# Block-sparse attention and a gated feed-forward layer in one kernel: another order of the same work

## The chip, the cores and the metric

The kernel runs on one core of a Trainium2 chip. Times are microseconds of device time; three runs are shown. In the tables PE is TensorE (PEld its weight loads), DVE is VectorE, ACT is ScalarE, POOL is GpSimd and SP is SyncE, which here issues every DMA.

## The reference

```python
# q, k, v: (8, 8, 576, 64); heads 0-3 local, heads 4-7 strided
scores = (q @ k.T) / sqrt(64)
rel = pos[:, None] - pos[None, :]
mask_local   = (rel >= 0) & (rel < 32)
mask_strided = (rel >= 0) & (pos[None, :] % 32 == pos[:, None] % 32)
scores = where(mask, scores, -1e9)
attn = exp(scores - max) / (sum(exp(scores - max)) + 1e-9)
x = (attn @ v).transpose(0, 2, 1, 3).reshape(4608, 512)
h = x @ w_in                                # 512 -> 2048
g = h * erf(softplus(h))
out = g @ w_out                             # 2048 -> 512
```

The inputs are float32; the weights reach the kernel as 64-bit words.

## The kernel before, in words

**The feed-forward part.** The 4608 tokens are cut into 12 chunks of 384, three for each pair of batches, and the 2048 hidden columns into 16 f-tiles of 128. `ftile(k)` is one f-tile of one chunk, k from 0 to 191. `mm1` (12 matmuls, L708) makes a 128 x 384 tile `h` in one of three PSUM buffers. The gate is evaluated by a chain that alternates between ScalarE and VectorE: `n1` (ScalarE), `n2` (VectorE, a<-h,a), `n3`, `n4` (ScalarE), `n5` (VectorE, a<-a,h), `n6` (VectorE, b<-b,a: both inputs in SBUF), `n7`, `gate` (ScalarE), `prod` (VectorE, h<-b,h), `split_hi` (ScalarE, ghi), `split_lo` (VectorE, glo, L749). After `split_lo` the h buffer is free. Three `mm2` (three matmuls each, L778) then add the f-tile's part to the outputs o0, o1 and o2; with the last f-tile of a chunk these are copied out and stored. A fp32 product is formed from high and low parts, so x, g and the weights are all kept as a pair. Names carry the f-tile's number: `glo_92` is the low part of f-tile 92.

**The attention part.** `piece` handles one pair of heads, one part j (0 to 2) of the sequence, for batches 0 and 1, whose work stands at the start. `quad` handles two pairs of heads for batches 2 to 7, and is named batch_headpair_j: 3_0_0 is batch 3, local heads, j = 0, and 5_2_0 is batch 5, strided heads, j = 0. I call them loc and str. A quad's scores (L484, 32 small matmuls in the trace) fill two PSUM banks; the banks have 384 columns in loc quads, 504 in str quads, and str quads with j = 2 have one bank of 288. For each bank: `mask` (VectorE, L502, one input in PSUM), `maxi` (GpSimd, an all-reduce over partitions, mx, L510), `sub` (VectorE, L517, sm<-sm,mx, both inputs in SBUF), `exp` (ScalarE, L524), `total` (GpSimd, all-reduce of sums, su, L530). The sums are transposed, inverted and spread by VectorE; `av` (x<-sm,v, TensorE, L574) needs the two `exp`; `scale`, `split_hi` and `split_lo_x` write the chunk's x.

**The order.** Nothing in the code above sets when an instruction stands where. Each op is added to a `Plan` with an engine, a cost in us, a key, the ops it follows and the buffers it uses. `Plan.order` is a list scheduler: for each engine it looks at the first WINDOW ops by key, finds when each could start, and takes the earliest, and among those about equally early the one with the lowest key. `new` buffers are taken from a pool of fixed depth, so an op that needs a buffer waits for the last user of the one that it replaces. Where TensorE would have nothing to do before the first mm1, a small `warm` matmul is put in. For the SBUF port that VectorE and GpSimd share the plan has a lock: a `sub`, an `n6` and some weight ops may not start while an op of GpSimd holds it, which is until its end less `FREED`:

```python
TWO = {"n6", "sub", "bits0", "bits1", "bits2", "split_lo_w"}
FREED = {"maxi": 0.75, "total": 0.95}
self.locks = eng == "pool" or eng == "dve" and emit.__name__ in TWO
```

The keys come from some 40 constants at the head of the file (SLOT is the key distance of f-tiles, MM2 the lag of mm2 in slots, W1K to W2S place the weights, A0 and A1 the pieces, QE, QO and QD the quads). The engines run the list in order, each waiting on semaphores where it needs another; the costs are of the plan alone.

**The weights.** w_in and w_out are loaded in 32 blocks (L653), and each is converted by three VectorE ops, a ScalarE copy and a VectorE subtraction. All of this is ahead of f-tile 16. `words8` to `words11` are the blocks that f-tiles 8 to 11 use.

Of the kernel before, what the change touches and what calls it, by code (L numbers as in the profile page):

```python
# [25 lines left out]
SW = 512  # L26


PRO = 78.728118
SLOT = 7.9300244  # L30
MM2 = 12.39792
W1K = (6.53644, 49.1778, -5.03539, 71.3026)
W1S = (5.65989, 16.7449, 3.18762, 26.1391)
W2K = 63.715556
W2S = 9.812094
A0K = -3.8060487
A0S = 1.2281868
A0D = 24.083007
A1K = 112.4806
A1S = -4.9858923  # L40
A1D = -8.5092613
QE = (12.856, 11.4352, 31.5648, 4.72851)
QO = (-4.21485, 2.52639)
QD = (0.348349, 1.45887, 1.7431, 1.71864, 1.13326)
ASH = 2.896798
ADT = 2.7828178
BACKLOG = 1.6450532

QL = 96
RB = 7  # L50
# [43 lines left out]

TWO = {"n6", "sub", "bits0", "bits1", "bits2", "split_lo_w"}

FREED = {"maxi": 0.75, "total": 0.95}


class Op:  # L100
# [9 lines left out]
class Plan:  # L110
# [5 lines left out]
    SAME = {"pe": 0.0, "act": 0.14, "dve": 0.13, "pool": 0.1, "sp": 0.0}  # L116
    LATENCY = {"pe": 0.25, "act": 0.2, "dve": 0.15, "pool": 0.6, "sp": 0.1}
    PATIENCE = 0.002
    WINDOW = 60

    def __init__(self, bufs):
        self.bufs, self.ops, self.filler = bufs, [], None
# [1 line left out]
    def add(self, eng, dur, key, emit, after=(), new=(), use=(), earliest=0.0):  # L124
        op = Op(eng, dur, key, emit, after, new, use, earliest)
        self.ops.append(op)
        return op
# [17 lines left out]
    def order(self):  # L145
# [4 lines left out]
        while left:  # L150
            best = None
            for e in self.ENGINES:
                can = [(o, n, self._ready(o, live)) for n, o in enumerate(queue[e][: self.WINDOW])]
                floor = max(free[e], dma - BACKLOG) if e == "sp" else free[e]
                port = held.get({"dve": "pool", "pool": "dve"}.get(e), 0.0)
# [34 lines left out]
def attention_moe(  # L190
# [37 lines left out]
    def buf(pool, tag, shape, name, dtype=F32):  # L228
        def make():
            return pools[pool].tile(shape, dtype, tag=tag, name=name, bufs=bufs[tag])  # L230

        return Buf(tag, make)

    def named(name, f):
        f.__name__ = name
        return f
# [178 lines left out]
    def quad(b, loc, j, key, dt, ring):  # L415
# [9 lines left out]
        cols = 4 * w // nbank  # L425
# [4 lines left out]
        sm = [buf("apool", "sm", [P, 512], f"sm{i}_{pid}") for i in range(nbank)]  # L430
        mx = [buf("apool", "mx", [P, 512], f"mx{i}_{pid}") for i in range(nbank)]
        su = [buf("apool", "mx", [P, 512], f"su{i}_{pid}") for i in range(nbank)]
# [95 lines left out]
        def total(k):  # L528
            def run():
                yield nc.gpsimd.partition_all_reduce(su[k][:, :cols], sm[k][:, :cols], P, ReduceOp.add)  # L530

            return named("total", run)
# [75 lines left out]
        add = plan.add  # L608
# [4 lines left out]
        o_e = []  # L613
        for k in range(nbank):
            o = add("dve", dve(cols), key + 0.1 + 0.01 * k, mask(k), [o_s], [], [s[k], sm[k]])
            o = add("pool", 0.4 + cols * 0.0028, key + 0.2 + 0.01 * k, maxi(k), [o], [mx[k]], [sm[k]], earliest=6.7)
            o = add("dve", dve(cols), key + QD[0] * dt + 0.01 * k, sub(k), [o], [], [mx[k], sm[k]])
            o_e.append(add("act", act(cols), key + QD[0] * dt + 0.1 + 0.01 * k, exp(k), [o], [], [sm[k]]))
        o_g = []
        for k in range(nbank):  # L620
            o = add("pool", 0.5 + cols * 0.005, key + QD[1] * dt + 0.01 * k, total(k), [o_e[k]], [su[k]], [sm[k]])
            o_g.append(o)
        n_g = (1 if pos == n else 2 * nblk) * 0.06 + width / 960.0 + (0.06 if pos > n else 0.0)
        o = None
        for h in range(2):
            k = h % nbank
            o = add("dve", n_g, key + QD[2] * dt + 0.01 * h, gather(h), [o_g[k]] + ([o] if o else []), [tt, inv] if h == 0 else [], [su[k], tt])
        o = add("dve", 0.36, key + QD[2] * dt + 0.05, invert, [o], [rc], [tt])
        o_i = add("dve", dve(width), key + QD[2] * dt + 0.06, spread, [o], [], [rc, inv])
        d_v = (1.2 if n > QL else 0.98) if nblk == 2 else 0.6  # L630
# [3 lines left out]
        for i in range(2):  # L634
            hi, lo = split(i)
            o = add("act", act(w, 0.06), key + QD[4] * dt + 0.1, hi, [o_x] + ring, [], [px])
# [57 lines left out]
    def ftile(k, ready):  # L694

        c, f = k // NFC, k % NFC
        v0 = PRO + SLOT * k
        ph = buf("ps_h", "h", [P, 512], f"h_{k}")
        a = buf("mpool", "a", [P, CH], f"a_{k}")
        bb = buf("mpool", "b", [P, CH], f"b_{k}")  # L700
        ghi = buf("mpool", "ghi", [P, CH], f"ghi_{k}", F32R)
# [49 lines left out]
        add = plan.add  # L751
        ta, tp, td = act(CH), act(CH, 0.05), dve(CH)

        def at(offset):
            return v0 + (offset + 0.3) * SLOT / 3.9

        first = add("pe", 2.09, v0, mm1, ready[0], [ph])
        o = add("act", tp, at(0.0), n1, [first], [a], [ph])
        o = add("dve", td, at(0.6), n2, [o], [], [ph, a])
        o = add("act", ta, at(1.2), n3, [o], [], [a])  # L760
        o = add("act", ta, at(2.25), n4, [o], [bb], [a])
        o = add("dve", td, at(2.9), n5, [o], [], [a, ph])
        o = add("dve", td, at(3.5), n6, [o], [], [a, bb])
        o = add("act", ta, at(4.35), n7, [o], [], [bb])
        o = add("act", ta, at(5.55), gate, [o], [], [bb])
        o = add("dve", td, at(6.2), prod, [o], [], [bb, ph])
        o_h = add("act", tp, at(6.8), split_hi, [o], [ghi], [ph])
        o_l = add("dve", td, at(7.9), split_lo, [o_h], [glo], [ph, ghi])
        last = []
        for t in range(NTT):  # L770
# [4 lines left out]
            def mm2(t=t, po=po):  # L775
# [7 lines left out]
            o = add(  # L783
                "pe", 0.693, v0 + MM2 * SLOT + 0.2 * t, mm2, [o_l] + ready[1] + ([order_o[t]] if f else []),
                [po] if f == 0 else [], [ghi, glo] + ([] if f == 0 else [po]),
            )
            order_o[t] = o
            last.append(o)
            if f == NFC - 1:
# [7 lines left out]

                o = add("act", act(DM, 0.06), v0 + 2.5 * SLOT + 0.7 + 0.2 * t, evac, [o], [ob], [po])
                add("sp", P * DM * 4 / 3.6e5, o.key + 0.1, store, [o], [], [ob])
# [17 lines left out]
    o = plan.add("sp", 0.6, -20.0, load_consts, new=[con_f])  # L817
# [2 lines left out]
    o_ps, order_o = [None] * NTT, [None] * NTT  # L820

    x_of = {}
    mm1_of, mm1_first = {}, []

    w1, w2, win, wout = [], [], [], []
    for f in range(0, DF, SW):
        for c in range(NCC):
            i = len(w1)
            rows, sl = slice(c * P, (c + 1) * P), slice(f, f + SW)
            op, pair = weight(i, w_in, rows, sl, W1K[i // 4] + W1S[i // 4] * (i % 4))  # L830
            w1.append(op)
            win.append(pair)
    for f in range(NFC):
        rows, sl = slice(f * P, (f + 1) * P), slice(0, DM)
        op, pair = weight(NFC + f, w_out, rows, sl, W2K + W2S * f)
        w2.append(op)
# [57 lines left out]
    first = plan.add("pe", 0.11, -10.0, warm, o_con, [warm_ps])  # L894
# [102 lines left out]
```

## Time and profile before

| | before |
|---|---|
| three runs, median (lowest to highest) | 976.35 us (975.68 to 977.12) |
| the profiled execution | 977.93 us |
| its span, first to last instruction | 976.2 us |
| PE busy | 950.1 us, 97% |
| DVE busy | 796.0 us, 82% |
| ACT busy | 652.8 us, 67% |
| POOL busy | 327.4 us, 34% |
| granted TensorE clock | 1.00 |
| DMA | 68.86 MB, most of it in the first 80 us |

Busy is time in which an engine has an instruction in it; a matmul that waits inside the pipeline is counted busy. The span is 1.7 us shorter than the profiled time, for what lies around it. In the rows that follow, "PEld h L708 <- DVE glo L749: total, times, longest" is a wait: who, at which line, waited for whom. A row of the timeline begins with the start and the length in us.

### The profile page before, as it was taken

How to read it: one execution, taken by the hardware profiler on the slowest of the kernel's cores; microseconds unless marked ns; L12 is line 12 of the kernel's file. 1: busy time of each engine (PE TensorE's matmuls, PEld its weight loads, DVE VectorE, ACT ScalarE, POOL GpSimd, SP SyncE). 2: the span in 40 equal slices, each digit the busy share in tenths (PEclk: the TensorE clock that was granted, in tenths of full speed). 3: DMA queues.
4: the chain of work that ended last, by engine and by line, in shares of the span. 5: the costliest groups of instructions: out<-in, count | busy, mean ns of one | idle time of the engine just before them, and what ended most of it. 6: DMA issues, size and time to landing. Idle time of an engine off the chain costs nothing.

```text
span 976.2 us, 16572 instructions
## 1 busy us (share of the span) xinstructions
PE 950.1 (97%) x6052; PEld 823.8 (84%) x6052; DVE 796.0 (82%) x1727; ACT 652.8 (67%) x1475; POOL 327.4 (34%) x160
## 2 busy tenths in 40 slices
PE   8999999999999999999999999999999999999998
PEld 6788888888878888888887888888887888999997
DVE  6999999787888887777888798778788888666664
ACT  3777777667667666667656766766766766766765
POOL 3533115234453552243454544313445344000000
PEclk9999999999999999999999999999999999999999
DMA  8994202112122121102121211111212210000000
GB/s 311 323 363 128 68 1 76 38 44 70 52 57 77 46 71 47 42 26 83 39 81 52 70 55 48 65 37 44 70 35 74 76 46 4 33 1 1 33 1 34
DMA packets 37666, 68.86 MB, mean 71 GB/s; under 512 B 4176, under 2 KB 18640, under 8 KB 37584
## 3 DMA queue, kind: packets, MB, share of 16 engines
q1 hardware_dynamic: 37584, 67.80, 21.6%
q8 instruction: 48, 0.79, 0.3%
q14 instruction: 34, 0.28, 0.1%
HBM read 58.34 MB, written 9.44 MB: 69 GB/s over the span
## 4 chain that ended last, share of the span: by engine, by line
PE 53%; DVE 32%; ACT 10%; issue 3%; DMA 2%; SPq 0%; DVEq 0%
PE h L708 25%; PE o L778 22%; DVE a L713 6%; DVE b L713 5%; DVE glo L749 4%; ACT b L716 4%; DVE h L743 3%; ACT a L716 3%; DVE sm L517 2%; PE x L574 1%; DVE sm L502 1%; PE s L484 1%; DVE tt L548 1%; DMA qk<-qk_loc 1%; DVE w L666 1%
## 5 line engine op out<-in xcount | busy, mean ns | idle before, releaser
L778 PE MATMUL o<-pair,ghi 128*128 128x512 f32 x1152 | 363.1, 396 | 0.0
L708 PE MATMUL h<-xhi,pair 128*128 128x384 f32 x1536 | 306.1, 341 | 13.1 <-DVE glo L749 12.6
L708 PEld LDWEIGHTS h<-xhi,pair 128*128 128x128 f32 x1536 | 266.4, 188 | 39.1 <-DVE glo L749 30.1
L716 ACT ACTIVATE b<-b 128x384 f32<-128x384 f32 x384 | 199.8, 524 | 83.9 <-DVE b L713 80.7
L778 PEld LDWEIGHTS o<-pair,ghi 128*128 128x128 f32 x1152 | 209.8, 188 | 39.9 <-issue 2.0
L778 PE MATMUL o<-pair,glo 128*128 128x512 f32 x576 | 224.6, 390 | 0.0
L510 POOL PARTITION_ALL_REDUCE mx<-sm x66 | 102.0, 1588 | 360.3 <-DVE sm L502 357.3
L530 POOL PARTITION_ALL_REDUCE su<-sm x66 | 183.4, 2807 | 66.8 <-ACT sm L524 66.8
L708 PE MATMUL h<-xlo,pair 128*128 128x384 f32 x768 | 164.5, 336 | 0.0
L716 ACT ACTIVATE a<-a 128x384 f32<-128x384 f32 x192 | 100.9, 525 | 77.3 <-DVE a L713 75.2
L713 DVE SCALAR_TENSOR_TENSOR a<-a,h 128x384 f32<-128x384 f32 x192 | 104.9, 546 | 52.8 <-ACT b L716 51.6
L749 DVE TENSOR_TENSOR glo<-h,ghi 128x384 fp32r<-128x384 f32 x192 | 105.2, 548 | 42.5 <-ACT ghi L746 41.4
L708 PEld LDWEIGHTS h<-xlo,pair 128*128 128x128 f32 x768 | 136.1, 188 | 0.0
L743 DVE TENSOR_TENSOR h<-b,h 128x384 f32<-128x384 f32 x192 | 105.8, 554 | 31.7 <-ACT b L716 31.1
L778 PEld LDWEIGHTS o<-pair,glo 128*128 128x128 f32 x576 | 108.2, 188 | 23.6
L713 DVE SCALAR_TENSOR_TENSOR b<-b,a 128x384 f32<-128x384 f32 x192 | 126.5, 660 | 1.8
L713 DVE SCALAR_TENSOR_TENSOR a<-h,a 128x384 f32<-128x384 f32 x192 | 105.4, 549 | 21.5 <-ACT a L716 20.8
L716 ACT ACTIVATE a<-h 128x384 f32<-128x384 f32 x192 | 93.0, 485 | 39.2 <-PE h L708 38.2
L746 ACT CAST ghi<-h 128x384 fp32r<-128x384 f32 x192 | 90.5, 472 | 38.3 <-DVE h L743 19.8
L716 ACT ACTIVATE b<-a 128x384 f32<-128x384 f32 x192 | 100.2, 522 | 2.9
L313 POOL PARTITION_ALL_REDUCE mx<-sm x24 | 41.7, 1739 | 65.5 <-ACT sm L305 62.0
L517 DVE TENSOR_TENSOR sm<-sm,mx 128x384 f32<-128x384 f32 (+2 forms) x66 | 52.1, 790 | 0.4
(53 smaller groups left out, 695.8 us busy)
## 6 DMA issues: line engine op xcount, KB each, us to landing
qk<-qk_loc SPq DMA_DIRECT2D x48, 304.0 KB, 3.3
qk<-qk_str SPq DMA_DIRECT2D x32, 380.0 KB, 3.7
v<-v_all SPq DMA_DIRECT2D x80, 130.0 KB, 2.2
out<-ob SPq DMA_DIRECT2D x36, 256.0 KB, 2.1
words<-w_in SPq DMA_DIRECT2D x16, 512.0 KB, 6.0
words<-w_out SPq DMA_DIRECT2D x16, 512.0 KB, 6.4
qk<-qk_str SPq DMA_DIRECT2D x16, 136.0 KB, 2.5
v<-v_all SPq DMA_DIRECT2D x16, 65.0 KB, 2.0
```

Of the source, the lines that this page charges most:

```text
L313: yield nc.gpsimd.partition_all_reduce(mx[:, :cols], sm[:, :cols], P, ReduceOp.max)
L484: yield nc.tensor.matmul(s[bank][cols_k, c : c + n], qk[i][rows, keys + part * 64 : keys + (part + 1) * 64], qk[i][rows, (blk * 2 + h) * n ...
L510: yield nc.gpsimd.partition_all_reduce(mx[k][:, :cols], sm[k][:, :cols], P, ReduceOp.max)
L517: yield nc.vector.tensor_tensor(out=d, in0=d, in1=mx[k][:, :cols], op=ALU.subtract)
L530: yield nc.gpsimd.partition_all_reduce(su[k][:, :cols], sm[k][:, :cols], P, ReduceOp.add)
L708: yield nc.tensor.matmul(ph[:, :CH], win[4 * s + cc][:, w, fs], x[cc][:, c0 : c0 + CH], start=(i == 0), stop=(i == len(terms) - 1))
L713: yield nc.vector.scalar_tensor_tensor(out=out, in0=in0, scalar=scalar, in1=in1, op0=op0, op1=op1)
L716: yield nc.scalar.activation(dst, src, func, bias=bias[i], scale=scale)
L743: yield nc.vector.tensor_tensor(out=ph[:, :CH], in0=bb.tile, in1=ph[:, :CH], op=ALU.mult)
L746: yield nc.scalar.copy(ghi.tile, ph[:, :CH])
L749: yield nc.vector.tensor_tensor(out=glo.tile, in0=ph[:, :CH], in1=ghi.tile.bitcast(F32), op=ALU.subtract)
L778: yield nc.tensor.matmul(po.tile, g[:, ts], wout[f][:, w], start=(f == 0 and i == 0), stop=(f == NFC - 1 and i == 2),)
```

## The change

Three things are edited, and all act through the order alone. The cost of `total` in the plan, and how early it gives up the port, are set anew. Two dependences are added to the plan: `mm1` of an f-tile follows the mm1 before it, and `split_hi` follows the split_hi before it. All key constants have new values, and the scheduler looks 70 ops ahead instead of 60. The instructions themselves are the same; line numbers from 757 on move by one or two.

```diff
-PRO = 78.728118
-SLOT = 7.9300244
-MM2 = 12.39792
+PRO = 78.092106
+SLOT = 5.9116753
+MM2 = 25.630719
...
-FREED = {"maxi": 0.75, "total": 0.95}
+FREED = {"maxi": 0.7, "total": 1.0}
...
-    WINDOW = 60
+    WINDOW = 70
...
-            o = add("pool", 0.5 + cols * 0.005, key + QD[1] * dt + 0.01 * k, total(k), [o_e[k]], [su[k]], [sm[k]])
+            o = add("pool", 0.094 + cols * 0.0063, key + QD[1] * dt + 0.01 * k, total(k), [o_e[k]], [su[k]], [sm[k]])
...
-        first = add("pe", 2.09, v0, mm1, ready[0], [ph])
+        first = add("pe", 2.09, v0, mm1, ready[0] + mm1_first[-1:], [ph])
...
-        o_h = add("act", tp, at(6.8), split_hi, [o], [ghi], [ph])
+        o_h = add("act", tp, at(6.8), split_hi, [o] + hi_of[-1:], [ghi], [ph])
+        hi_of.append(o_h)
...
-    mm1_of, mm1_first = {}, []
+    mm1_of, mm1_first, hi_of = {}, [], []
```

What it moves, at three places. On VectorE, around the two `sub` of quad 5_2_0 (`sm0` and `sm1` are its two banks), before:

```order
L713 SCALAR_TENSOR_TENSOR a_93_5947<-a_93_5947,h_93_5914 128x384
L517 TENSOR_TENSOR sm0_5_2_0_5892<-sm0_5_2_0_5892,mx0_5_2_0_5939 128x504
L713 SCALAR_TENSOR_TENSOR b_93_5970<-b_93_5970,a_93_5947 128x384
L749 TENSOR_TENSOR glo_92_5998<-h_92_5831,ghi_92_5994 128x384
L517 TENSOR_TENSOR sm1_5_2_0_5893<-sm1_5_2_0_5893,mx1_5_2_0_5963 128x504
L604 TENSOR_TENSOR xlo2_82<-x_4_2_2_5942,xhi2_78 128x18x4
```

and in the changed kernel:

```order
L713 SCALAR_TENSOR_TENSOR b_94_5997<-b_94_5997,a_94_5978 128x384
L517 TENSOR_TENSOR sm0_5_2_0_5960<-sm0_5_2_0_5960,mx0_5_2_0_6000 128x504
L749 TENSOR_TENSOR glo_93_6037<-h_93_5908,ghi_93_6033 128x384
L517 TENSOR_TENSOR sm1_5_2_0_5961<-sm1_5_2_0_5961,mx1_5_2_0_6017 128x504
L743 TENSOR_TENSOR h_94_5939<-b_94_5997,h_94_5939 128x384
```

The `n6` (b<-b,a) that stood between the subs now stands ahead of the first, and one row is left between them.

On TensorE, ahead of the `av` of quad 3_0_1 (x_3_0_1): before, the last rows of the second of two mm1 (f-tile 51) stand there, behind two mm1 and five mm2 after the quad's scores:

```order
L708 MATMUL h_51_3659<-xlo0_80,pair0_293 128x384
L708 MATMUL h_51_3659<-xlo1_81,pair1_329 128x384
L708 MATMUL h_51_3659<-xlo2_82,pair2_383 128x384
L708 MATMUL h_51_3659<-xlo3_83,pair3_420 128x384
L574 MATMUL x_3_0_1_3680<-sm0_3_0_1_3579,v0_3_0_1_3394 64x96
```

and in the changed kernel, after one mm2, the mm1 of f-tile 50 and these five mm2 behind the scores:

```order
L708 MATMUL h_50_3619<-xlo3_83,pair3_523 128x384
L779 MATMUL o1_2_2847<-pair30_1920,ghi_46_3537 128x512 x2
L779 MATMUL o1_2_2847<-pair30_1920,glo_46_3540 128x512
L779 MATMUL o2_2_2876<-pair30_1920,ghi_46_3537 128x512 x2
L779 MATMUL o2_2_2876<-pair30_1920,glo_46_3540 128x512
L779 MATMUL o0_2_2837<-pair31_1972,ghi_47_3605 128x512 x2
L779 MATMUL o0_2_2837<-pair31_1972,glo_47_3608 128x512
L779 MATMUL o1_2_2847<-pair31_1972,ghi_47_3605 128x512 x2
L779 MATMUL o1_2_2847<-pair31_1972,glo_47_3608 128x512
L779 MATMUL o2_2_2876<-pair31_1972,ghi_47_3605 128x512 x2
L779 MATMUL o2_2_2876<-pair31_1972,glo_47_3608 128x512
L574 MATMUL x_3_0_1_3679<-sm0_3_0_1_3586,v0_3_0_1_3260 64x96
```

The `av` has moved ahead of the mm1 of f-tile 51 and stands closer to its scores.

On SP, at the start of the program, before:

```order
L806 DMA con_f_87<-consts 128x446
L653 DMA words8_89<-w_in 128x1024
L268 DMA qk_0_0_0_91<-qk_loc 128x608
L275 DMA v_0_0_0_93<-v_all 128x260
L268 DMA qk_0_1_0_95<-qk_loc 128x608
L275 DMA v_0_1_0_97<-v_all 128x260
L653 DMA words9_101<-w_in 128x1024
```

and in the changed kernel:

```order
L807 DMA con_f_87<-consts 128x446
L268 DMA qk_0_0_0_89<-qk_loc 128x608
L275 DMA v_0_0_0_91<-v_all 128x260
L268 DMA qk_0_1_0_93<-qk_loc 128x608
L275 DMA v_0_1_0_95<-v_all 128x260
L275 DMA v_0_0_1_97<-v_all 128x260
L653 DMA words11_101<-w_in 128x1024
```

The first block of weights has moved behind the inputs of two pieces and the v of a third. The pieces of batch 1, which were spread over f-tiles 0 to 10, j = 2 first, are now spread over f-tiles 0 to 15, j = 0 first. On TensorE the last rows, from the mm1 of f-tile 158 on, stand as before.

More of the change, by code (lines that the diff above doesn't have):

```diff
@@ L26 @@
 SW = 512
-PRO = 78.728118
-SLOT = 7.9300244
-MM2 = 12.39792
[L32 to L47, printed above, removed]
+PRO = 78.092106
+SLOT = 5.9116753
+MM2 = 25.630719
+W1K = (30.3392, 45.2407, 29.777, 74.3109)
+W1S = (6.66747, 15.6958, -3.12843, 8.62929)
+W2K = 80.64347
+W2S = 6.6022671
+A0K = 0.61635903
+A0S = 4.0703236
+A0D = -2.7259218
+A1K = 77.691688
+A1S = 7.4559608
+A1D = -4.9661421
+QE = (13.0906, 7.59449, 28.6735, 3.97592)
+QO = (-2.73583, 2.28537)
+QD = (0.569358, 2.08749, 1.61931, 1.79434, 1.13453)
+ASH = -0.34305701
+ADT = -0.58951321
+BACKLOG = 1.9815506
 QL = 96
```

## The prediction

> **What bounds the kernel now.** I read the page's first part, then the windows by stage, then the waits, then the timeline at the longest waits.
>
> ```profile
> PE 950.1 (97%) x6052; PEld 823.8 (84%) x6052; DVE 796.0 (82%) x1727; ACT 652.8 (67%) x1475; POOL 327.4 (34%) x160
> 0.00:50.40 50.40, 45.27 (x322) 35.55 (x322) 41.07 (x89) 28.61 (x84) 23.09 (x17) 1.00 0.93 319
> 50.40:150.00 99.60, 96.59 (x596) 84.32 (x596) 99.33 (x228) 74.29 (x170) 26.33 (x16) 1.00 0.40 134
> 200.00:826.00 626.00, 613.26 (x4089) 527.59 (x4088) 524.97 (x1151) 412.33 (x926) 258.12 (x121) 1.00 0.18 55
> ...
> 50.37 0.95 PE L708 MATMUL h<-xhi,pair 128*128 128x384 f32 x4
> ```
>
> The columns of the windows are length, then busy time of PE, PEld, DVE, ACT and POOL, granted clock, DMA share, GB/s. TensorE is the engine that sets the time, in three stages. Until the first mm1 (50.37), the DMA queues (0.93) and VectorE prepare weights. Until 150 us VectorE is never idle (99.33 of 99.6 us). From 200 to 826 us, f-tiles and quads mixed, VectorE works 84% of the time and nothing but TensorE is full. So what an order of work can win is TensorE's waiting. These are its waits from 150 to 826 us, and the first row for 50 to 150 us:
>
> ```profile
> PEld h L708 <- DVE glo L749: 2.6, 6, 0.8
> ...
> PEld h L708 <- DVE glo L749: 27.5, 46, 1.7
> PEld x L574 <- ACT sm L524: 2.6, 5, 0.7
> ```
>
> The weight load of the next mm1 waits 27.5 us in all for `split_lo` (glo), the last op on an h buffer: there are three h buffers, so mm1 of f-tile k+3 waits until the chain of f-tile k has ended. Why is that chain late? Two VectorE ops have a long tail, the others none:
>
> ```profile
> L713 DVE SCALAR_TENSOR_TENSOR a<-h,a x192: 494/551/559, 53.8 to 962.9; 128x384 f32<-128x384 f32 x192
> L713 DVE SCALAR_TENSOR_TENSOR b<-b,a x192: 493/551/2564, 57.0 to 966.4; 128x384 f32<-128x384 f32 x192
> L517 DVE TENSOR_TENSOR sm<-sm,mx x66: 457/559/2647, 144.3 to 817.2; 128x384 f32<-128x384 f32 x36, 128x504 f32<-128x504 f32 x24, 128x288 f32<-128x288 f32 x6
> ...
> L713 DVE SCALAR_TENSOR_TENSOR b<-b,a 128x384 f32<-128x384 f32 x192 | 126.5, 660 | 1.8
> ```
>
> Minimum, median and maximum: `n6` (b<-b,a) and `sub` (sm<-sm,mx) reach 2.6 us where their medians are 0.55. Both read two SBUF tiles; `n2` (a<-h,a) has one input in PSUM and stays at 0.559. The timeline shows what holds them, in quad 3_2_0 (batch 3, strided heads, j=0) and then 4_2_0:
>
> ```profile
> 282.39 0.68 DVE L517 TENSOR_TENSOR sm<-sm,mx 128x504 f32<-128x504 f32 x1
> 283.92 2.65 DVE L517 TENSOR_TENSOR sm<-sm,mx 128x504 f32<-128x504 f32 x1
> 283.82 3.19 POOL L530 PARTITION_ALL_REDUCE su<-sm  x1 [2.27 <-ACT sm L524]
> 287.28 1.08 PE L574 MATMUL x<-sm,v 128*64 128x126 f32 x14 [0.41 <-ACT sm L524]
> ...
> 426.28 6.52 POOL L530 PARTITION_ALL_REDUCE su<-sm  x2 [1.11 <-ACT sm L524]
> 426.50 2.56 DVE L713 SCALAR_TENSOR_TENSOR b<-b,a 128x384 f32<-128x384 f32 x1
> 429.58 1.67 PE L708 MATMUL h<-xhi,pair 128*128 128x384 f32 x8 [1.40 <-DVE glo L749]
> ```
>
> In 3_2_0 the second `sub` comes 0.10 us after GpSimd began the first `total` and takes 2.65 us instead of 0.68. In 4_2_0 an `n6` comes 0.22 us after it and takes 2.56; the mm1 behind its chain then waits 1.40 us. So a VectorE op with two SBUF inputs that is issued behind a running all-reduce stands still, and everything behind it in VectorE's queue with it. The plan knows this lock, but the old cost of `total` is too short: 0.5 + 504 x 0.005 = 3.02 us against 3.19 to 3.26 here (6.52 for two). The new 0.094 + 504 x 0.0063 gives 3.27.
>
> The Trainium skill's page "SBUF — State Buffer", section "Who interferes with whom", says the same and more: an op with two SBUF inputs contends with a GpSimd op that reads SBUF, and the second to issue is blocked for the whole instruction. The trace agrees on who is blocked, not on how long: the `sub` of 3_2_0 ends at 286.57, 0.44 us before the all-reduce's record does. By the page the stall of 4_2_0 that is kept below would cost up to 0.4 us more, a sum of 965.4.
>
> **The change, part by part.** No instruction changes its kind or shape and none is added but for one warm matmul fewer (131, filler where TensorE has nothing to do), so only waits can move. The sum is made against the profiled execution (977.9 us; span 976.2), 1.6 us above the median of 976.35; I take the waits from the one and apply them to the other.
>
> *The second `sub` stands closer to the first.* The order shows it quad by quad. Where the old order has two rows between the subs of the first loc and str quads of an odd batch (3_0_0, 3_2_0, 5_0_0, 5_2_0, 7_0_0, 7_2_0) and of 4_0_1 and 6_0_1, the new one has none or one in five of the eight, an `n6` of its own in 6_0_1, and glo and prod in 3_2_0 and 7_2_0. mm1's waits around those quads, by window: 262 to 297, 495 to 530 and 727 to 763 us (the first row again) for the odd batches; 400 to 403 and 632 to 635 (one row, twice) for 4_0_1 and 6_0_1; 196 to 198, 428 to 431 and 660 to 663 (one row, three times) for the `n6` of 2_2_0, 4_2_0 and 6_2_0; and 350 to 363, 582 to 596 and 815 to 827 for the loc quad j=2 of odd batches:
>
> ```profile
> PEld h L708 <- DVE glo L749: 3.7, 5, 1.1
> PEld h L708 <- DVE glo L749: 3.6, 4, 1.1
> ...
> PEld h L708 <- DVE glo L749: 0.7, 1, 0.7
> ...
> PEld h L708 <- DVE glo L749: 1.7, 1, 1.7
> ...
> PEld h L708 <- DVE glo L749: 1.5, 3, 0.7
> PEld h L708 <- DVE glo L749: 1.6, 3, 0.7
> PEld h L708 <- DVE glo L749: 1.4, 3, 0.6
> ```
>
> I let go the first group (3.7 + 3.6 + 3.7 = 11.0 us), with its three waits of x on exp (0.41 each, 1.2), the second (2 x 0.7 = 1.4), and two of the three 1.7 (3.4): in 4_2_0 the new order puts an `n6` and the second sub six and seven rows behind the first, where `total` runs. The fourth group (4.5) I keep: there the new order is not plainly better. Gone: 17.0 us.
>
> *What is late next: the x matmuls.* The new order starts `av` (x, L574) much sooner behind the scores. Between them the old order has 7.6 us or more of TensorE work in all but two of the loc quads (7.1 there), the new 6.2 to 6.6 us in ten: at 3_0_1 one mm1 of 2.08 us (303.27 to 305.35 below) and six mm2 of 0.68 (289.09 to 289.78 is one) instead of two and five. What must fit is mask, max, sub and exp:
>
> ```profile
> 298.87 0.89 PE L484 MATMUL s<-qk 64*64 64x96 f32 x32
> 303.27 1.55 PE L708 MATMUL h<-xhi,pair 128*128 128x384 f32 x8
> 305.35 1.55 PE L708 MATMUL h<-xhi,pair 128*128 128x384 f32 x8
> 302.76 0.87 DVE L713 SCALAR_TENSOR_TENSOR b<-b,a 128x384 f32<-128x384 f32 x1
> 305.07 0.53 ACT L524 ACTIVATE sm<-sm 128x384 f32<-128x384 f32 x1
> ...
> 488.88 0.89 PE L484 MATMUL s<-qk 64*64 64x96 f32 x32
> 497.16 0.52 ACT L524 ACTIVATE sm<-sm 128x384 f32<-128x384 f32 x1 [1.79 <-DVE sm L517]
> ...
> 289.09 0.62 PE L778 MATMUL o<-pair,ghi 128*128 128x512 f32 x2
> 289.78 0.62 PE L778 MATMUL o<-pair,ghi 128*128 128x512 f32 x2
> ```
>
> From the end of the scores to the end of the second exp it took 305.60 - 299.76 = 5.8 us in 3_0_1 without a `total` in the way, and 497.68 - 489.77 = 7.9 us in 5_0_0, whose second sub was stalled. So each of the ten costs between 0 and 1.7 us (7.9 - 6.2). Subs that stand together are nearest to 3_0_1; I take 0.3 each, 3.0 us, range 0 to 17.
>
> *mm1 triples that stand tight.* Counting the rows by the same durations, ten f-tiles of the mixed stage in the new order have only 8.2 to 8.5 us of TensorE work before the mm1 three further on, against four before. Bounds for the six more: 0, and twice the 0.7 us wait above. In the old order f-tiles 64 and 112 are such places, and their windows (378 to 388 and 610 to 621 us) have this row each:
>
> ```profile
> PEld h L708 <- DVE glo L749: 0.2, 1, 0.2
> ```
>
> So nearer to the low end: 0.35 each, 2.1 us.
>
> *The start.* SP issues five loads of q, k and v ahead of the first weight, which moves from the second to the seventh DMA. VectorE's four ops on that weight filled 4.88 to 8.13 us and now come later:
>
> ```profile
> 4.88 0.43 DVE L659 TENSOR_SCALAR w<-words 128x512 uint32<-128x512 uint32 x1 [0.86 <-DMA words<-w_in]
> 7.44 0.69 DVE L680 TENSOR_TENSOR pair<-w,pair 128x512 fp32r<-128x512 f32 x1 [0.68 <-ACT pair L677]
> ```
>
> That is up to 2.3 us (their busy time) of a queue that is full until 150 us. In that stage batch 1's pieces are spread to f-tile 15 instead of 10. By back-to-back times VectorE's queue ahead of glo holds 2 to 4 us less at f-tiles 5 to 10 and 2 us more at 16, and TensorE has about 2 us more of its own work behind it there. mm1's waits on glo of that stage (2.6 us) may go. Between -2.6 and +2.3 I take +0.5. SP is in order, and later loads stand where they stood to within a few of its rows. The last 34 f-tiles have the same order on TensorE; they change nothing.
>
> Sum: -17.0 + 3.0 + 2.1 + 0.5 = -11.4; 976.35 - 11.4 = 965.0 us.
>
> **Rivals.** *Slower: x takes over.* If the subs are held up all the same (by an `n6` behind the max all-reduce, which the new order still has ahead of most first subs), each x waits as 5_0_0's chain says, and TensorE with it: 1.7 us in the ten, 17.0, and 3_2_0's 0.41 in the twelve large str quads, whose cover falls to 7.6 to 8.8 us in most, 4.9. Then -17.0 + 21.9 + 2.1 + 0.5 = +7.5, 983.9 us. With the ten alone it ends slower from (17.0 - 2.6) / 10 = 1.4 us each. Against it: in 3_0_1 such an `n6` (302.76) took 0.3 us too long and the chain still took 5.8.
>
> *The order misses by a hair.* In 3_2_1 a second sub with glo and prod ahead of it started before `total`, and took 0.68:
>
> ```profile
> 324.87 0.68 DVE L517 TENSOR_TENSOR sm<-sm,mx 128x504 f32<-128x504 f32 x1
> 324.93 6.83 POOL L530 PARTITION_ALL_REDUCE su<-sm  x2 [1.63 <-ACT sm L524]
> ```
>
> 0.06 us decided. The new 3_2_0, 6_2_0 and 7_2_0 have that pattern; if they fall on the wrong side, three waits of about 3.7, 1.7 and 3.7 us come back: 974.1 at most, 969.6 if half does.
>
> *No change.* New waits of x and h eat the gain without exceeding it (the ten at the 1.4 us above): 974.4 to 978.3 us.
>
> **How the numbers follow.** Forecast with its own spread (956 to 970): 0.60. By a hair: 0.18, faster. No change: 0.09, mostly within 0.2%. Slower by x: 0.13. A measurement of this kernel can tell 0.2%, 2 us. Faster 0.78, same 0.08, slower 0.14. The low end, 955: the kept 4.5 and the start's 2.6 also go, and the new waits halve. The high end, 978: the ten a little over 1.4 us.
>
> **What would show it.** Right: the maxima of `sub` fall under 1 us in most quads, and the h wait's 27.5 us to about 14 (27.5 - 15.8 + 2.1); x's 2.6 us may grow by 4. Wrong: `n6` or `sub` again at 2.6 us ten times a period, or x waiting over 15 us; or the first mm1 later than 52 us. If the h wait falls and the time doesn't, the x rows or the weight loads must hold the difference.

## The result and the profile after

| | before | after |
|---|---|---|
| median (lowest to highest), four runs each on one chip | 976.74 us (975.68 to 977.28) | 961.93 us (961.01 to 962.93) |
| ratio, with its 95% interval | | 0.9843 (0.9828 to 0.9857) |
| the profiled execution, its span | 977.93 us, 976.2 us | 962.17 us, 960.4 us |

The new order is 14.8 us faster; 11.4 were forecast. First the page's busy times, then the windows by stage (columns as before), then two waits of TensorE's weight loads from 150 to 826 us, on `split_lo` and on exp:

```profile
PE 941.6 (98%) x6051; PEld 824.5 (86%) x6051; DVE 779.3 (81%) x1727; ACT 652.8 (68%) x1475; POOL 325.7 (34%) x160
0.00:50.40 50.40, 45.16 (x328) 36.76 (x329) 38.84 (x90) 30.15 (x88) 19.97 (x17) 1.00 0.95 333
50.40:150.00 99.60, 94.12 (x604) 81.86 (x603) 99.24 (x229) 72.38 (x163) 30.67 (x16) 1.00 0.41 135
200.00:826.00 626.00, 623.26 (x4176) 545.24 (x4175) 518.04 (x1166) 424.53 (x955) 257.29 (x120) 1.00 0.18 55
...
PEld h L708 <- DVE glo L749: 11.6, 26, 1.3
PEld x L574 <- ACT sm L524: 2.6, 7, 0.5
```

VectorE does the same 1727 instructions in 16.7 us less (796.0 to 779.3): that is time it stood still. In the mixed stage TensorE is now busy 623.26 of 626 us (613.26 before), and the wait for `split_lo` falls from 27.5 to 11.6 us. The wait of x on exp stays at 2.6. The two operations with the long tail, by their least, middle and greatest ns:

```profile
L517 DVE TENSOR_TENSOR sm<-sm,mx x66: 417/560/2644, 127.6 to 801.9; 128x384 f32<-128x384 f32 x36, 128x504 f32<-128x504 f32 x24, 128x288 f32<-128x288 f32 x6
L713 DVE SCALAR_TENSOR_TENSOR b<-b,a x192: 495/552/2374, 57.2 to 950.6; 128x384 f32<-128x384 f32 x192
```

The tail isn't gone: one `sub` of 2.64 us is left, and `n6` of up to 2.37. Where in the execution did the time go? The starts of mm1 cut it into stretches that compare: f-tiles are all alike, and each pair of batches brings the same quads. The timeline's first matmuls of f-tiles 48, 144 and 191, of before and then of after:

```profile
292.88 0.79 PE L708 MATMUL h<-xhi,pair 128*128 128x384 f32 x3 [0.22 <-DVE glo L749]
757.81 0.96 PE L708 MATMUL h<-xhi,pair 128*128 128x384 f32 x4 [0.19 <-DVE glo L749]
959.97 1.20 PE L708 MATMUL h<-xhi,pair 128*128 128x384 f32 x6
```

```profile
293.38 0.95 PE L708 MATMUL h<-xhi,pair 128*128 128x384 f32 x4
744.20 1.12 PE L708 MATMUL h<-xhi,pair 128*128 128x384 f32 x5
944.17 1.03 PE L708 MATMUL h<-xhi,pair 128*128 128x384 f32 x5
```

From f-tile 48 to 144 (two pairs of batches) before takes 464.9 us and after 450.8: 14.1 us of the 15.8 between the spans. From 144 to 191 it is 202.2 and 200.0 (2.2 us). Up to f-tile 48 after is 0.5 us later: it reaches f-tile 32 at 216.0 against 212.7 and makes 2.8 good by f-tile 48. So the start costs 3.3 us and the mixed stage gives 19.1. The table holds all kernels that were run, by these stretches (the profiled execution of each) and by the median; the ratio is to the kernel before on the same chip.

| kernel | f-tile 16 | f-tile 32 | 48 to 144 | f-tile 191 | median us | ratio (interval) |
|---|---|---|---|---|---|---|
| before | 139.5 | 212.7 | 464.9 | 960.0 | 976.74 | |
| after | 143.1 | 216.0 | 450.8 | 944.2 | 961.93 | 0.9843 (0.9828 to 0.9857) |
| before_no_total | 138.3 | 209.8 | 450.2 | 937.7 | 955.90 | 0.9787 (0.9766 to 0.9807) |
| after_no_total | 141.4 | 212.2 | 447.8 | 936.5 | 956.16 | 0.9782 (0.9764 to 0.9800) |
| before_subs_together | 138.4 | 211.6 | 458.3 | 949.4 | 967.79 | 0.9904 (0.9886 to 0.9921) |
| after_subs_together | 145.3 | 218.1 | 451.1 | 946.7 | 963.59 | 0.9861 (0.9843 to 0.9880) |
| total_cost_alone | 138.8 | 211.7 | 462.4 | 955.6 | 973.82 | 0.9959 (0.9945 to 0.9974) |
| costs_old_keys | 138.5 | 211.4 | 457.3 | 951.2 | 970.79 | 0.9924 (0.9906 to 0.9943) |
| keys_old_cost | 143.2 | 216.4 | 465.9 | 966.0 | 980.14 | 1.0028 (1.0016 to 1.0039) |
| after_weight_first | 144.9 | 217.7 | 450.7 | 945.9 | 963.77 | 0.9857 (0.9843 to 0.9872) |
| after_one_swap | 142.3 | 215.1 | 450.6 | 943.0 | 960.95 | 0.9838 (0.9824 to 0.9851) |
| after_old_start | 147.2 | 219.8 | 449.6 | 946.7 | 966.06 | 0.9884 (0.9869 to 0.9900) |
| after_batch1_early | 148.9 | 221.1 | 449.3 | 947.8 | 966.04 | 0.9882 (0.9867 to 0.9897) |
| after_quad_later | 139.7 | 214.7 | 449.6 | 941.7 | 959.67 | 0.9816 (0.9802 to 0.9829) |

One execution stands for each kernel, and executions differ. The start of after and after_one_swap is the same order, and f-tile 16 comes 0.9 us apart; from 48 to 144 after and after_weight_first are the same order and 0.1 us apart. The execution of costs_old_keys is the fastest of its four (967.84 us), that of keys_old_cost the second slowest of its ten (982.34).

### The profile page after: what moved, and what is told of

Read it like the earlier page. It is cut to its first block, busy times and chain, and to the rows that moved or that the text cites. A ratio compares the mean times of both kernels' runs of the same rounds, so it can differ in the third digit from the quotient of the medians.

```text
span 960.4 us, 16592 instructions
## 1 busy us (share of the span) xinstructions
PE 941.6 (98%) x6051; PEld 824.5 (86%) x6051; DVE 779.3 (81%) x1727; ACT 652.8 (68%) x1475; POOL 325.7 (34%) x160
## 2 busy tenths in 40 slices
DMA packets 37666, 68.86 MB, mean 72 GB/s; under 512 B 4176, under 2 KB 18640, under 8 KB 37584
## 4 chain that ended last, share of the span: by engine, by line
PE 76%; DVE 18%; ACT 3%; issue 2%; DMA 1%; SPq 0%; DVEq 0%; ACTq 0%
PE h L708 34%; PE o L779 34%; DVE a L713 3%; PE s L484 2%; PE x L574 2%; DVE b L713 2%; DVE glo L749 2%; ACT b L716 2%; DVE w L672 1%; DVE pair L680 1%; DVE w L666 1%; DVE h L743 1%; DMA qk<-qk_loc 1%; ACT a L716 1%; DVE sm L517 1%
## 5 line engine op out<-in xcount | busy, mean ns | idle before, releaser
L530 POOL PARTITION_ALL_REDUCE su<-sm x66 | 181.2, 2783 | 54.3 <-ACT sm L524 50.0
L713 DVE SCALAR_TENSOR_TENSOR b<-b,a 128x384 f32<-128x384 f32 x192 | 122.7, 639 | 2.1
L517 DVE TENSOR_TENSOR sm<-sm,mx 128x384 f32<-128x384 f32 (+2 forms) x66 | 45.1, 690 | 0.5 <-POOL mx L510 0.4
```

Of the source, the lines that this page charges most:

```text
L517: yield nc.vector.tensor_tensor(out=d, in0=d, in1=mx[k][:, :cols], op=ALU.subtract)
L713: yield nc.vector.scalar_tensor_tensor(out=out, in0=in0, scalar=scalar, in1=in1, op0=op0, op1=op1)
```

## The experiments

**Is it the lock of `total` at all?** In both orders the 66 all-reduces of `total` became a memset on GpSimd (0.42 us in the middle), so the sums are left out and everything else stands where it stood:

```diff
-                yield nc.gpsimd.partition_all_reduce(su[k][:, :cols], sm[k][:, :cols], P, ReduceOp.add)
+                yield nc.gpsimd.memset(su[k][:, :cols], 1.0)
```

> The kernel before, its order unchanged, with each of the 66 GpSimd all-reduces of the sums (total) replaced by a GpSimd memset of the same tile, which reads nothing; the sums are left out, so x is not normalised. Lock theory (what the change won is VectorE ops with two SBUF inputs no longer standing behind a running total): the long sub and n6 go, mm1's wait on glo falls from 27.5 us to 12 or less between 150 and 826 us, and the time falls by 14 to 20 us, to 957 to 963. Rival (the change won by where it puts scores, x and mm2 on TensorE, and the stalls were mostly covered): the stalls go, the time falls by 4 us or less.

> The changed kernel with the same replacement; the sums are left out. Lock theory: little is left to win, because the new order already keeps sub and n6 away from total: 1 to 4 us less than 961.9, and the two kernels without total end within 5 us of each other, with before's the faster by up to 4 us, since its start loses less. Rival: both kernels win alike, and the distance of about 15 us between the two orders stays.

The two orders tie, 955.90 and 956.16 us. The 14.8 us between them are gone with `total`: the old order loses 20.8 us to it, the new one 5.8, each about 1 to 2 us more than the expectations say. VectorE's busy time falls to 770.4 and 766.2 us, by 25.6 and 13.1. The tie hides two smaller differences. Up to f-tile 32 before_no_total is 2.4 us ahead; from there to f-tile 191 it takes 727.9 us and after_no_total 724.3 (747.3 and 728.2 with `total`). So 15.5 of the 19.1 us of the mixed stage go with `total`, and 3.6 are won by the new order without it. These are the h wait of before_no_total, its `sub` and `n6`, and the h wait of after_no_total:

```profile
PEld h L708 <- DVE glo L749: 8.9, 23, 0.8
L517 DVE TENSOR_TENSOR sm<-sm,mx x66: 457/550/1182, 143.1 to 794.9; 128x384 f32<-128x384 f32 x36, 128x504 f32<-128x504 f32 x24, 128x288 f32<-128x288 f32 x6
L713 DVE SCALAR_TENSOR_TENSOR b<-b,a x192: 494/549/1450, 55.8 to 944.1; 128x384 f32<-128x384 f32 x192
```

```profile
PEld h L708 <- DVE glo L749: 5.3, 18, 0.5
```

No `sub` or `n6` takes over 1.5 us any more; what is left of the tail (1182 and 1450 ns) is the lock of the other all-reduce, `maxi`: in before_no_total the twelve `sub` and `n6` over 0.95 us from 150 us on all begin while a `maxi` runs. The memset also leaves GpSimd idle longer (174.7 us busy for 327.4). That did not shorten the stalls behind `maxi`: from f-tile 48 to 144 they are 10 in both, 6.5 us in before and 6.3 here.

**Is it where the second `sub` stands?** In the kernel before, the second `sub` was put right behind the first in the eight quads of the prediction's first two groups, and in the kernel after in all 30 quads with two banks:

```diff
+    ops = plan.order()
+    for pid in ('3_0_0', '3_2_0', '4_0_1', '5_0_0', '5_2_0', '6_0_1', '7_0_0', '7_2_0'):
+        _, one, max2, two = sub_of[pid][:4]
+        ops.remove(two)
+        ops.insert(max(ops.index(one), ops.index(max2)) + 1, two)
```

> The kernel before with one edit of its order: in quads 3_0_0, 3_2_0, 4_0_1, 5_0_0, 5_2_0, 6_0_1, 7_0_0 and 7_2_0 the second sub is issued right behind the first on VectorE, ahead of the two ops that stood between. Lock theory, by the prediction's terms: the waits of those quads go, 11.0 + 1.4 + 1.2 = 13.6 us, less what the n6 and split_lo that now come later cost (up to 0.7 us each): 962 to 967 us. Rival: two subs earlier by a microsecond change nothing, 975 to 978.

> The changed kernel with the second sub right behind the first in all 30 quads that have two. Lock theory: the one long sub that is left (6_2_0, 2.64 us) goes and with it the wait of the mm1 of f-tile 122 (1.3 us); elsewhere nothing was stalled, so 959.5 to 962. Rival: the searched order is disturbed and new waits come: over 963.

In before it brought 9.0 us (967.79, 0.8 above the expected range), and no `sub` is over 0.698 us; the `n6` keeps its 2.56. The first row here is `sub`, the second `n6` (L718 in this kernel):

```profile
L517 DVE TENSOR_TENSOR sm<-sm,mx x66: 457/551/698, 143.2 to 806.6; 128x384 f32<-128x384 f32 x36, 128x504 f32<-128x504 f32 x24, 128x288 f32<-128x288 f32 x6
L718 DVE SCALAR_TENSOR_TENSOR b<-b,a x192: 493/551/2560, 55.9 to 955.8; 128x384 f32<-128x384 f32 x192
```

So the position of eight subs is worth more than half of the change. In after the same rule brought nothing (963.59 us, 48 to 144 in 451.1 against 450.8): the one long `sub` went and an `n6` of 2.56 us appeared a little behind it. Its f-tile 16 comes 2.2 us later; the time is the rival's.

**The planner's cost, or the new keys?** Two more orders come from parts of the change: the old kernel with the new cost of `total` only (the diff), and the new kernel with the old keys, whose edit also sets WINDOW back to 60. A third is the new kernel with the old cost:

```diff
-            o = add("pool", 0.5 + cols * 0.005, key + QD[1] * dt + 0.01 * k, total(k), [o_e[k]], [su[k]], [sm[k]])
+            o = add("pool", 0.094 + cols * 0.0063, key + QD[1] * dt + 0.01 * k, total(k), [o_e[k]], [su[k]], [sm[k]])
```

> The kernel before with one number pair changed: the planner's cost of a total (0.094 + 0.0063 per column in place of 0.5 + 0.005); keys, FREED, the turn rule and the window stay old. The order changes only through it: no n6 stands between the two subs of any quad any more (six have none, fourteen one row, seven two, three three; before seventeen have two and five hold an n6). Theory A (what counts is whether VectorE's queue puts a two-SBUF-input op under a running total; the corrected cost does that by itself): 963 to 969 us, h wait from 150 us on 15 to 20 us, the n6 maximum still over 1.4 for the max all-reduce. Rival B (the searched keys bring the gain; the cost alone only shuffles rows): 974 to 978 us, h wait 24 to 29 us.

> The kernel after with the old keys of the order (all the numbers from PRO to BACKLOG); new total cost, new FREED, in turn and window as after. Theory A (the cost and the lock's end carry the mixed stage, the keys only the start and details): 961 to 968 us, h wait from 150 us on 12 to 19 us. Rival B (the keys carry it): 971 to 977 us, h wait over 22 us. Both expect the start as before: the first weight's ops at 4.9 us and the mm1 of f-tile 16 near 139.5.

> The kernel after with the old cost of a total; new keys, FREED, turn and window stay. Nine quads have their subs next to each other, nine one row between, three two and nine three. Theory A (cost carries it): much of the gain goes, 968 to 977 us, h wait from 150 us on 20 to 28 us. Rival B (the keys carry it): 960 to 965 us, h wait 10 to 17 us.

Neither theory holds. total_cost_alone and costs_old_keys miss the ranges of theory A by 5 and 3 us and lie 0.2 us below rival B's; keys_old_cost lies far outside rival B's 960 to 965 and 3 us above theory A's. Their h waits from 150 us on, 24.2, 17.6 and 25.8 us, lie in the ranges of B, A and A. From f-tile 48 to 144: old keys and old cost 464.9 us; new cost 457.3 (with FREED; 462.4 with the cost alone); new keys 465.9; both 450.8. The new keys without the cost are slower than before, the cost without the keys brings 7 us, both together 14.8. With the new keys the cost is needed, and it isn't enough: with it and the old keys some `n6` still fall behind a `total`, as f-tile 75's in the timeline of total_cost_alone, 0.22 us late, and f-tile 103's, 0.07 us late:

```profile
424.53 2.56 DVE L713 SCALAR_TENSOR_TENSOR b<-b,a 128x384 f32<-128x384 f32 x1
424.31 3.35 POOL L530 PARTITION_ALL_REDUCE su<-sm  x1 [1.12 <-ACT sm L524]
560.90 2.55 DVE L713 SCALAR_TENSOR_TENSOR b<-b,a 128x384 f32<-128x384 f32 x1
560.83 3.19 POOL L530 PARTITION_ALL_REDUCE su<-sm  x1 [0.34 <-ACT sm L524]
```

What the keys add doesn't show in the plan's length. By the plan's own start times, which are sums of its costs and no measurement, f-tiles 48 to 144 take 448.1 us in total_cost_alone and in costs_old_keys and 448.2 in after; the chip takes 462.4, 457.3 and 450.8. These three reckon with the new cost, and they are equally good if every op comes when it was planned; they differ in what happens when it doesn't. (The 448.1 of before and the 448.8 of keys_old_cost are sums with the old cost, which is too short, and don't compare.) How the keys were chosen isn't shown here. The two new dependences and WINDOW = 70 do nothing in the new kernel: with the dependences left out of it, or put alone into the old one, or with 60 for 70, the list of instructions is the same row for row.

**Fewer stalls, or better covered ones?** The table counts, from f-tile 48 to 144, the `n6` and `sub` that begin while a `total` runs and take over 0.2 us longer than usual, and adds up what they take too long. (In keys_old_cost the clock also fell twice in this stretch.)

| kernel | such ops | VectorE loses, us | 48 to 144, us |
|---|---|---|---|
| before | 13 | 17.3 | 464.9 |
| before_subs_together | 7 | 7.7 | 458.3 |
| total_cost_alone | 15 | 20.6 | 462.4 |
| costs_old_keys | 14 | 17.4 | 457.3 |
| keys_old_cost | 16 | 20.9 | 465.9 |
| after | 8 | 7.6 | 450.8 |

The change halves what VectorE loses, but the time doesn't follow that sum alone. before_subs_together loses as much as after and takes 7.5 us longer; total_cost_alone loses more than before and takes 2.5 us less. Without `total` the stretch takes 450.2 us in the old order and 447.8 in the new. So 17.3 us of stalls cost 14.7 us in before, 7.7 cost 8.1 in before_subs_together, and 7.6 cost 3.0 in after: the new order also lets TensorE feel less of the stalls that are left. Which of its moves does that (the place of mm1, mm2 and av on TensorE is the first suspect) no run here separates.

**The start.** Up to f-tile 32 the new order loses 3.3 us. Is it the first weight, whose ops on VectorE now begin at 8.66 us?

```diff
...
+    loads = [o for o in ops if o.eng == "sp"]
+    first = next(o for o in loads if o.new[0].tag.startswith("w"))
+    ops.remove(first)
+    ops.insert(ops.index(loads[0]) + 1, first)
```

> The kernel after with the first weight load moved up to be SyncE's second DMA, as in the kernel before; the rest of the order stays. Theory A (the start's loss is the idle time of VectorE's first weight ops): these ops begin near 4.9 us in place of 8.7, the mm1 of f-tile 16 comes up to 2.3 us sooner than 143.1, and the time falls 0.5 to 2.5 us, to 959.4 to 961.5. Rival B (the loss comes from batch 1's pieces spread to f-tile 15, with VectorE's last xlo and pairs late there): the early ops are early, the mm1 of f-tile 16 stays within 0.7 us of 143.1, time within 0.7 us of after's 961.9.

No. The ops begin at 5.15 us and the first mm1 comes 1.75 us later, at 51.23 for 49.48, and all that follows is as much later: f-tile 16 comes at 144.9 and the time is 963.77, outside the ranges of both theories. This is the first weight op in after, and in after_weight_first with the next weight's behind it:

```profile
8.66 0.54 DVE L659 TENSOR_SCALAR w<-words 128x512 uint32<-128x512 uint32 x1 [4.84 <-DMA words<-w_in]
```

```profile
5.15 0.43 DVE L659 TENSOR_SCALAR w<-words 128x512 uint32<-128x512 uint32 x1 [1.10 <-DMA words<-w_in]
10.19 0.57 DVE L659 TENSOR_SCALAR w<-words 128x512 uint32<-128x512 uint32 x1 [3.88 <-DMA words<-w_in]
```

VectorE now waits 3.88 us for the second weight. The DMA queues are 0.92 to 0.95 busy up to 50.4 us in these orders, and moving one load up moves others down. (Two words ahead of the prediction are too sharp. VectorE's last op on a weight begins at 148.3 us in before and 153.3 in after, so the weights aren't all done ahead of f-tile 16. And the first 80 us of before move 319 GB/s, some 26 of the 68.86 MB, which isn't most of it.) Then the pieces of batch 1, spread to f-tile 15 by the new keys; two other starts, which leave VectorE's order from about its row 390 on as it is in after. Of the first, the keys of batch 1:

```diff
...
-A1K = 77.691688
-A1S = 7.4559608
-A1D = -4.9661421
+A1K = 103.3
+A1S = -3.72
+A1D = -6.3
...
```

> The kernel after with the start's keys of before (A0K, A0S, A0D as they were; A1K, A1S, A1D, W2K, W2S scaled to the new SLOT: 103.3, -3.72, -6.3, 66.9, 7.31). From VectorE's row 390 or so on the order is that of after, so the mixed stage stays. Theory A (batch 1's pieces spread to f-tile 15 cost the start's 5 us): the mm1 of f-tile 16 comes 2 to 4 us sooner than 143.1, TensorE's loss between f-tiles 16 and 29 falls from 5.8 to under 2, and the time falls 2 to 5 us, to 957 to 960. Rival B (VectorE is full until f-tile 25 whatever the order of the start, because the new order puts batch 2's quads earlier): f-tile 32 within 1.5 us of after's 216.0 or later, time 961 to 965.

> The kernel after with other start keys (W1K, W1S, W2K, W2S, A0*, A1*): batch 1's pieces run early and in falling order, as in before, and the first mm1 is issued sooner; from VectorE's row 390 or so on the order is that of after. Theory A (the start's loss is its own): the first mm1 at 47 to 49 us, f-tile 16 at 139 to 141, f-tile 32 at 212 to 214.5, time 958 to 960.5. Rival B (VectorE's work up to f-tile 32 sets it): whatever the first mm1 gains is lost by f-tile 32, which stays within 1 us of 216.0; time 961 to 963.

The first also edits the keys of batch 0 and of w_out, the second those of w_in as well. Both are slower by 4 us. Theory A fails: f-tile 32 comes at 219.8 and 221.1. Rival B allows that in the first run, but not in the second (216.0 within 1), and its times (961 to 965, 961 to 963) are too low. The second one starts mm1 at 44.94 us, 4.5 before after, and TensorE then has so little to do that its clock falls to a half. Its windows of 4 us (the clock is the figure before the last two):

```profile
56.00:60.00 4.00, 1.61 (x12) 1.46 (x13) 3.84 (x10) 3.11 (x9) 0.88 (x1) 0.91 0.94 289
60.00:64.00 4.00, 3.03 (x12) 1.90 (x12) 3.13 (x9) 1.60 (x4) 1.42 (x1) 0.50 0.99 368
64.00:68.00 4.00, 2.56 (x7) 1.58 (x7) 3.02 (x9) 0.83 (x3) 0.16 (x1) 0.50 0.93 319
68.00:72.00 4.00, 3.66 (x16) 3.32 (x17) 3.14 (x10) 2.48 (x6) 1.60 (x1) 0.50 0.76 258
```

Last, what VectorE does ahead of f-tile 16. In the trace of after it has done all 12 instructions of quad 2_0_0 by then, from the first `mask` at 124.06 us to the last `split_lo_x` at 140 (4.6 us by the plan's costs; the expectation below counts 8 ops), where the old order has done one. That quad was moved back:

```diff
+                if b == 2 and i == 0:
+                    slot += 2.0
```

> The kernel after with one quad planned two slots later: 2_0_0, the first quad of batch 2, goes from ahead of the mm1 of f-tile 16 to behind it, while VectorE still prepares weights. Before f-tile 16's mm1 VectorE then has 1 to 3 of that quad's ops in place of 8; VectorE's order changes from row 229 to about 390 and is that of after behind it. Theory A (the start's 5 us come from this quad standing in VectorE's queue while it is full): f-tile 16's mm1 at 139 to 141 in place of 143.1, TensorE's loss from f-tile 16 to 28 under 3 us in place of 5.8, f-tile 32 at 213 to 215, time 958.5 to 961. Rival B (VectorE's work is only deferred, and TensorE waits for it a little later): f-tile 32 within 0.7 us of 216.0 and the time within 1 us of after's.

f-tile 16 comes at 139.7, f-tile 32 at 214.7, and the time is 959.67 us: all in theory A's ranges, and f-tile 32 and the time outside rival B's. But of the 3.4 us won at f-tile 16 only 1.3 are left at f-tile 32 and at f-tile 48 (292.1; 293.4 in after, 292.5 in after_one_swap, which has after's start). Most of the gain is given back, and that is rival B's mechanism. The time is the lowest of the kernels that compute everything; about 1.2 us of that comes from 48 to 144, where its order is that of after. Part of the giving back is the clock's: mm1 of f-tile 16 waits 2.51 us for `split_lo`, and from 140 to 144 us the granted clock is 0.64. So the start's 3.3 us stay without a settled cause. The runs speak against the first weight. They don't exclude the pieces of batch 1, since the two starts that moved them also lost clock; they show that moving them forward is no cure.

**One stall, by hand.** Quad 6_2_0 is where the prediction's rival "by a hair" came true. Its second `sub` begins 0.10 us behind `total`:

```profile
630.57 1.51 DVE L517 TENSOR_TENSOR sm<-sm,mx 128x504 f32<-128x504 f32 x1
632.93 2.64 DVE L517 TENSOR_TENSOR sm<-sm,mx 128x504 f32<-128x504 f32 x1
632.83 3.19 POOL L530 PARTITION_ALL_REDUCE su<-sm  x1 [0.55 <-ACT sm L524]
```

The order of VectorE was changed in one place, this `sub` ahead of the `prod` that stands before it:

```diff
+    two = sub_of["6_2_0"][3]
+    ops.remove(two)
...
+    ops.insert(ops.index(prod), two)
```

> The kernel after with two neighbouring rows of VectorE exchanged, once: in quad 6_2_0 the second sub goes ahead of the prod of f-tile 119 instead of behind it, so it is issued at about 632.5 instead of 632.93, before the total that begins at 632.83. Theory A (the port decides by which of the two starts first): this sub takes 0.68 us in place of 2.64, the mm1 of f-tile 122 loses 0 in place of 1.35 us, no later stall takes its place, and the time falls 1.0 to 1.5 us, to 960.4 to 961. Rival B (the stall moves on to the next VectorE op with two SBUF inputs, the n6 at 638, or total starts sooner and meets the sub all the same): time within 0.4 us of after's.

The `sub` takes 0.67 us as planned, both totals now follow each other without a gap, and the next `n6` falls behind them. In after_one_swap (`n6` is L718):

```profile
631.50 0.67 DVE L517 TENSOR_TENSOR sm<-sm,mx 128x504 f32<-128x504 f32 x1
635.77 2.04 DVE L718 SCALAR_TENSOR_TENSOR b<-b,a 128x384 f32<-128x384 f32 x1
631.86 6.52 POOL L530 PARTITION_ALL_REDUCE su<-sm  x2 [0.56 <-ACT sm L524]
```

From f-tile 118 to 128 it takes 45.66 us against 45.84: rival B. The time, 960.95 us, is below after's by 1.0, in theory A's range, but the f-tile 16 of its profiled execution is already 0.8 us early, and the intervals of the ratios overlap. In after_quad_later the same rows, in the old sequence, meet no stall there and the stretch takes 44.39:

```profile
630.41 0.67 DVE L517 TENSOR_TENSOR sm<-sm,mx 128x504 f32<-128x504 f32 x1
632.38 0.68 DVE L517 TENSOR_TENSOR sm<-sm,mx 128x504 f32<-128x504 f32 x1
632.44 3.66 POOL L530 PARTITION_ALL_REDUCE su<-sm  x1 [1.63 <-ACT sm L524]
```

Here the second `sub` is 0.06 us ahead of `total`, and it is `total` that takes longer, 3.66 us for 3.19. The two executions part a step before: an `n6` came 0.07 us behind the second `maxi` (in after 0.24 ahead of it), took 1.45 us, and the first `sub` behind it was free.

## Why the prediction was right, and where it was off

The direction and the mechanism were right: VectorE ops with two SBUF inputs under a running `total` were what the old order lost most by. The runs without `total` show it: the two orders tie, and 15.5 of the 19.1 us behind f-tile 32 are gone. The other 3.6 have another cause, which no run here names. The sizes were off in two places, with opposite signs, so that -11.4 lies nearer to -14.8 than its parts do to theirs; that is luck.

*Gone (-17.0), new waits of x (+3.0), tight mm1 (+2.1): -11.9 together; measured behind f-tile 32: -19.1.* Three terms were mis-sized:

- The fourth group, the loc quads j = 2 of odd batches, was kept at 4.5 us because "the new order is not plainly better" there. It went as well. The h waits of after around those quads (336 to 362, 568 to 590, 798 to 822 us) add up to 1.0:

```profile
PEld h L708 <- DVE glo L749: 0.3, 1, 0.3
PEld h L708 <- DVE glo L749: 0.4, 1, 0.4
PEld h L708 <- DVE glo L749: 0.3, 1, 0.3
```

- Of the three waits of 1.7 us, that of 4_2_0 was kept, because an `n6` and the second `sub` stand six and seven rows behind the first `sub`, and those of 2_2_0 and 6_2_0 were let go. It came out the other way round. At 4_2_0 VectorE first waits for ScalarE (the `n5` of 407.18, 1.15 us), so `n6` and `sub` come when `total`, from 405.15 to 408.34, lets go, and 0.5 us of mm1's wait is left:

```profile
407.18 0.55 DVE L713 SCALAR_TENSOR_TENSOR a<-a,h 128x384 f32<-128x384 f32 x1 [1.15 <-ACT b L716]
405.15 3.19 POOL L530 PARTITION_ALL_REDUCE su<-sm  x1 [1.40 <-ACT sm L524]
408.12 0.55 DVE L713 SCALAR_TENSOR_TENSOR b<-b,a 128x384 f32<-128x384 f32 x1
408.58 0.68 DVE L517 TENSOR_TENSOR sm<-sm,mx 128x504 f32<-128x504 f32 x1
```

  At 2_2_0 an `n6` comes 0.25 us behind `total`, and mm1 waits 1.34 us, the longest wait of the new order; at 6_2_0 mm1 waits 0.90:

```profile
180.16 6.36 POOL L530 PARTITION_ALL_REDUCE su<-sm  x2 [3.09 <-ACT sm L524]
180.41 2.37 DVE L713 SCALAR_TENSOR_TENSOR b<-b,a 128x384 f32<-128x384 f32 x1
183.30 1.35 PEld L708 LDWEIGHTS h<-xhi,pair 128*128 128x128 f32 x8 [1.34 <-DVE glo L749]
641.49 1.34 PEld L708 LDWEIGHTS h<-xhi,pair 128*128 128x128 f32 x8 [0.90 <-DVE glo L749]
```

  So of the 3.4 us that the three were to give, about 2.4 came (5.1 less 0.5, 1.3 and 0.9), and not where they were expected. The step that failed was counting VectorE's rows back to back. Rows tell what stands behind what, and a wait for another engine between them can put an op past the lock.
- x was to grow by 3.0 us and stayed at 2.6. In the trace of after the chain from the scores to the second exp takes 5.8 us in 3_0_1 again. From 200 us on it takes 5.6 to 6.5 us in twelve loc quads and 7.0 to 8.0 in four, and no wait of x is over 0.5 us; of the range 0 to 17 the low end was right.

For the h wait 13.8 us (27.5 - 15.8 + 2.1) was expected and 11.6 came. That is 15.9 less than before; the other 3.2 of the 19.1 stand in no single row, and where they went is open.

*The start (+0.5); measured to f-tile 32: +3.3.* The first mm1 did come sooner (49.48 for 50.37), and the 2.3 us for the late first weight were none, as after_weight_first shows. But VectorE's queue "2 us more at f-tile 16" with as much TensorE work to cover it was read as a draw. TensorE's f-tile 16 came 3.6 us later.

*The rivals.* "By a hair" came true in one of its three quads, 6_2_0. From f-tile 118 to 128 it costs 1.45 us (45.84 against the 44.39 of after_quad_later), less than the 1.7 set for it. "x takes over" did not happen: x waited 2.6 us and not 15. The Trainium skill's page "SBUF — State Buffer", section "Who interferes with whom", has the rule that the second op is blocked for the whole instruction. Here the `sub` of 6_2_0 ends at 635.57, and the all-reduce's record at 636.02: the trace has 0.45 us less than the rule, as in the row of the prediction (0.44).

## What to carry to other kernels

When an order of work is the change, ask of each shared port or lock which op would be issued behind its holder, and by how much: here 0.06 to 0.1 us of luck decides over 2 us. A plan's own length doesn't tell good orders from bad ones once they are equally tight (448.1 to 448.2 us planned, 450.8 to 462.4 measured). Count the stalls, but look at what they cost the engine that sets the time: 7.6 us of stalls cost 3.0 us in one order, 7.7 cost 8.1 in another. Take the resource out of the kernel altogether (here `total`) to learn what all orders together can still win. And a lone repair of one stall can hand it to the next op in the queue, so look at the whole stretch and not at the op.

## What the hardware showed that was not expected

A TensorE that waits a little over 2 us can pay twice. In keys_old_cost an `n6` under a `total` (2.56 us) delayed mm1 by 2.04 us at 242.6, and the granted clock of the next 4 us was 0.59; the same happened at 475 and 708 us. First the mm1, whose two parts take 1.55 and 0.86 us elsewhere, then the windows:

```profile
242.62 1.94 PE L708 MATMUL h<-xhi,pair 128*128 128x384 f32 x8 [2.04 <-DVE glo L749]
244.36 1.49 PE L708 MATMUL h<-xlo,pair 128*128 128x384 f32 x4
...
240.00:244.00 4.00, 1.96 (x17) 1.72 (x14) 3.83 (x9) 1.82 (x4) 4.00 (x2) 0.98 0.33 100
244.00:248.00 4.00, 4.00 (x13) 3.54 (x13) 1.58 (x5) 1.27 (x3) 2.15 (x2) 0.59 0.00 0
```

It isn't so in every execution: of that kernel's ten runs the two with a mean clock of 0.999 or more took 978.7 and 978.9 us, the four at 0.995 took 981.2 to 983.1. In before and after, whose longest waits are 1.7 and 1.3 us, no window of the mixed stage is below 1.00. The Trainium skill's page "TensorE: Matmul & The Clock Gate", section "Part 1: The HAM clock gate (the "warmup" mystery)", says that the clock is halved after an idle window of about 3.4 us, and that the windows run freely. The half agrees (0.50 in after_batch1_early). The length does not: 2.04 us of idling in a row were enough here, beside matmuls on both sides.
